# Attention with a window, then a gated convolution: another written-out order, convolution forms and PSUM banks, with ten masks on GpSimd and all but eight turns of x by DMA

## The chip, the cores and the metric

The kernel runs on one core of a Trainium2 chip. The metric is the device time of one execution in microseconds, lower is better; several executions are timed and the median counts. The engines are TensorE (PE), VectorE (DVE), ScalarE (ACT), GpSimd (POOL), and SyncE (SP), which issues nearly all DMAs here.

## The reference

Eight batches, eight heads, 576 rows, head width 64, in float32. Attention sees 32 rows to each side; its output goes into a feed-forward layer with a convolution of three taps as gate.

```python
scores = np.matmul(q, k.transpose(0, 1, 3, 2)) / np.sqrt(D)
mask = np.abs(pos[:, None] - pos[None, :]) <= 32
attn = softmax(np.where(mask, scores, -1e9))
x = np.matmul(attn, v)                       # then heads side by side: [8, 576, 512]
h = np.maximum(x @ w_in, 0.0)                # 512 -> 1024
conv = sum(conv_w[k] * hp[:, k:k + S, :] for k in range(3))   # per column, rows shifted by one
out = (h * sigmoid(conv)) @ w_out            # 1024 -> 512
```

## The kernel before

There is no loop nest and no scheduler at run time. A long string, `ORDER`, lists some 870 words, and each word calls one small function that records its instructions. The instructions of each engine run in the order in which they were recorded; semaphores hold an instruction back until its inputs are there and its buffer is free. All instructions are recorded through one helper, so nearly every row of the profile carries its line, L189; the tiles' names tell the steps apart.

A word is a step, its arguments, an engine letter (a ACT, d DVE, p POOL, t the SP queue) and, behind @, its PSUM banks. Attention works on a batch b, a half G of the heads and a half h of the rows (h=0 has four tiles of 64 rows, h=1 five):

- `lq`, `lk`, `lv` load q, k and v by SP; `cq`, `ck`, `cv` cast them to bf16 (tiles st to qb, vst to ve); `tq`, `tk` turn q and k on DVE; `vo` copies v shifted by 64 rows (ve to vo), on DVE, ACT or the queue.
- `sc` makes scores in PSUM. With the letter m the mask is added by eight more matmuls from the tile band; otherwise `mk` multiplies the exponentials by a 0/1 mask, on DVE (d) or POOL (p). `ex` is the exponential on ACT, two for each `sc`. `av` multiplies by v, `nr` normalises on DVE into xn.
- x must be turned for the next matmul: `xp` turns a block of 128 rows on PE and `xe` copies it out of PSUM, or `xt` turns it by a DMA on SP's queue.

The feed-forward part works on pieces P = 0 to 13: pieces 0 to 3 are half-width (192 rows), 4 to 13 full-width (384 rows), three to a pair of batches. In each piece m2 = 0 to 3 names a pair of 128-column groups:

- `ph` is the matmul with w_in (8 matmuls), `re` the ReLU on ACT into hT.
- `pc` starts the convolution in one of several forms. P: six matmuls with diagonal weights. A, D, S: twelve matmuls on quarter arrays. X: two scaled copies on ACT, and then `tp` adds the other two taps in four DVE instructions on the tile z. Y: half on PE, half on DVE.
- `th` is the tanh on ACT, to z in SBUF (second letter z) or in place in PSUM; `ga` multiplies by h on DVE into gT. `sw` moves halves for form S.
- `py` is the matmul with w_out (8 matmuls), `ye` copies y out of PSUM, `st` stores it.

The first feed-forward step needs attention's first batch; from there on attention of later batches and pieces of earlier ones are interleaved in `ORDER`. xT, turned x, has two buffers, each for a pair of batches; vst is one buffer for each block of v; z has four pairs of buffers.

Of the kernel before, what the change touches and what calls it, by code (L numbers as in the profile page):

```python
# [35 lines left out]
av,0,1,1@2 xe,0,0,d av,0,0,1@4 lv,1,0 ci,0,p nr,0,1,1 ph,0,2@0 ph,0,1@1 nr,0,0,1 re,0,2 lo,0 ci,3,p ph,0,0@2 re,0,1
pc,0,2,Pz@0 re,0,0 xp,0,3@1 lk,2,0 cq,1,0,p th,0,2,Pz pc,0,1,A@2 xp,0,2@4 xe,0,3,a ga,0,2,Pz ph,0,3@0 xe,0,2,a
pc,0,0,Pz@1 th,0,1,A lo,3 ck,1,0,p tq,1,0 ph,1,3@4 re,0,3 ga,0,1,A ph,1,0@5 th,0,0,Pz lq,2,0 cq,1,1,p tk,1,0 re,1,3
ph,1,2@6 re,1,0 xp,0,4@4 ga,0,0,Pz ph,1,1@5 re,1,2 lo,2 ck,1,1,p tq,1,1 xe,0,4,a sc,1,0,0,m@6+0 re,1,1 pc,1,2,P@4 lo,1
ex,1,0,0,1 cv,1,2,p tk,1,1 pc,0,3,P@5 ex,1,0,0,0 ph,2,3@0 th,1,2,P lk,2,1 cv,1,1,p th,0,3,P ga,1,2,P sc,1,1,0,d@6+2  # L40
lq,2,1 cv,1,0,a ph,2,2@1 ga,0,3,P ex,1,1,0,1 vo,1,0,d pc,1,3,Pz@4 re,2,3 ex,1,1,0,0 ph,2,1@5 lv,1,4 co,0,d re,2,2
av,1,0,0@6 th,1,3,Pz sc,1,1,1,m@0+2 mk,1,1,0,d re,2,1 pc,2,2,Pz@4 lv,1,3 ck,2,0,a ga,1,3,Pz nr,1,0,0 pc,1,1,Pz@5
th,2,2,Pz tk,2,0 th,1,1,Pz lq,3,0 co,3,p av,1,1,0@6 pc,2,3,P@4 ex,1,1,1,0 pc,1,0,P@5 ex,1,1,1,1 nr,1,1,0 ph,2,0@0
th,2,3,P lk,3,1 cq,2,0,p s6 th,1,0,P ga,1,1,Pz xp,1,0@6 xp,1,1@7 re,2,0 xe,1,0,a sc,1,0,1,m@0+2 lv,2,1 ga,2,3,P
xe,1,1,a pc,2,1,Y@6 ga,1,0,P co,2,a ph,3,3@4 ga,2,2,Pz lq,3,1 co,1,p tq,2,0 pc,2,0,Y@5 ex,1,0,1,1 ph,3,1@7 ex,1,0,1,0
tp,2,1,Y ph,3,2@2 re,3,3 lv,2,0 ck,2,1,p re,3,1 tp,2,0,Y py,0,2@4 th,2,1,Y re,3,2 ga,2,1,Y th,2,0,Y tk,2,1 lk,3,0
cq,2,1,p pc,3,3,Az@6 lk,4,0 pc,3,1,Dz@0 ye,0,2,a ga,2,0,Y cv,1,4,p py,0,1@2 th,3,1,Dz tq,2,1 th,3,3,Az lv,2,2 cv,1,3,p
ga,3,1,Dz vo,1,1,a sc,2,0,0,m@4+0 py,0,0@3 lv,2,3 cq,3,0,p ye,0,1,d ga,3,3,Az ex,2,0,0,1 lq,4,1 av,1,1,1@6 tq,3,0
ck,3,1,a py,1,0@2 st,0,1 cv,2,1,p nr,1,1,1 ex,2,0,0,0 ye,0,0,a av,1,0,1@0 tk,3,1 ye,1,0,a sc,2,0,1,d@4+6 st,0,0
cq,3,1,p ph,3,0@3 ex,2,0,1,0 nr,1,0,1 lv,2,4 pc,3,2,Pz@2 ex,2,0,1,1 re,3,0 sc,2,1,0,d@4+6 tq,3,1 th,3,2,Pz xp,1,2@0  # L50
st,1,0 ck,3,0,p xp,1,3@1 ex,2,1,0,0 xp,1,4@2 ex,2,1,0,1 pc,3,0,Pz@3 xe,1,3,d xe,1,2,a sc,2,1,1,m@4+6 mk,2,1,0,d
xe,1,4,a lk,4,1 tk,3,0 th,3,0,Pz ph,4,0@0 ex,2,1,1,1 lq,4,0 cv,2,2,p ga,3,2,Pz cv,2,0,a ex,2,1,1,0 ph,4,1@2 lv,3,0
ga,3,0,Pz ck,4,0,a mk,2,0,1,d py,1,2@4 re,4,0 tk,4,0 lv,3,2 cq,4,1,p re,4,1 lq,5,0 cv,2,3,a pc,4,0,A@0 tq,4,1 vo,2,0,t
ye,1,2,a ph,4,3@2 th,4,0,A cv,2,4,d lv,3,3 vo,2,1,d pc,4,1,P@4 lv,3,4 re,4,3 ga,4,0,A av,2,0,1@6 th,4,1,P pc,4,3,Az@2
st,0,2 ck,4,1,p nr,2,0,1 ph,4,2@0 th,4,3,Az ga,4,1,P lk,5,0 cq,4,0,p py,1,1@6 tk,4,1 re,4,2 lv,3,1 cv,3,0,p tq,4,0
pc,4,2,Pz@4 lk,5,1 cv,3,2,a ye,1,1,a ga,4,3,Az av,2,1,1@0 th,4,2,Pz sc,3,0,1,d@2+6 st,1,1 cq,5,0,p nr,2,1,1 ex,3,0,1,1
lv,4,0 av,2,1,0@4 ex,3,0,1,0 ga,4,2,Pz xp,2,4@0 xp,2,2@1 xe,2,4,a sc,3,1,1,m@2+6 xt,2,3 cv,3,3,p nr,2,1,0 py,2,0@0
ex,3,1,1,0 xe,2,2,d cv,3,4,a lv,4,2 mk,3,0,1,d ex,3,1,1,1 st,1,2 av,2,0,0@4 vo,3,1,d py,2,1@1 ye,2,0,a lv,4,3 ck,5,0,p
nr,2,0,0 lv,4,4 cv,3,1,a xp,2,0@0 ye,2,1,a xp,2,1@2 vo,3,0,d sc,3,0,0,d@4+6 xe,2,0,a py,2,2@3 xe,2,1,a tq,5,0 lk,6,1
ck,5,1,p ex,3,0,0,0 lk,6,0 ex,3,0,0,1 tk,5,0 sc,4,1,1,m@4+0 lv,4,1 cv,4,0,p ye,2,2,a av,3,1,1@6 mk,3,0,0,d lq,6,0  # L60
# [5 lines left out]
lv,5,2 lq,6,1 sc,4,0,0,d@0+6 ph,6,0@2 re,6,1 lv,6,0 ex,4,0,0,1 ex,4,0,0,0 ph,6,2@4 ga,5,1,Dz lv,5,1 cv,5,3,p re,6,0
st,2,2 th,5,2,Xz pc,5,3,Az@6 re,6,2 ph,7,0@0 lv,6,3 mk,4,0,0,d th,5,3,Az ga,5,2,Xz pc,6,0,Az@2 lv,5,4 ph,7,1@4 tq,5,1
re,7,0 th,6,0,Az lk,7,0 pc,6,2,D@0 ga,5,3,Az ph,7,2@6 tk,6,0 lq,7,0 cv,5,2,p re,7,1 pc,6,1,A@2 th,6,2,D ga,6,0,Az
py,3,0@4 re,7,2 lv,6,2 cq,6,1,p ga,6,2,D th,6,1,A pc,6,3,Az@6 py,3,1@5 ye,3,0,d th,6,3,Az ga,6,1,A st,3,0 pc,7,0,Dz@0
tq,6,0 ye,3,1,a sc,4,1,0,m@2+6 th,7,0,Dz cv,5,4,p py,3,2@4 st,3,1 ga,6,3,Az ex,4,1,0,1 vo,5,1,t ex,4,1,0,0 tq,6,1  # L70
ck,7,0,p sc,5,0,1,m@6+0 lv,6,4 ye,3,2,a av,4,1,1@2 tk,6,1 ex,5,0,1,0 cq,7,1,p st,3,2 ph,7,3@4 ex,5,0,1,1 nr,4,1,1
cq,7,0,p pc,7,1,Az@0 re,7,3 av,4,1,0@6 ck,7,1,d xt,4,3 av,4,0,0@2 th,7,1,Az py,4,1@4 cv,6,3,p nr,4,1,0 xt,4,2 cv,6,0,a
cv,5,1,d sc,5,1,1,m@0+6 nr,4,0,0 cv,6,4,p ye,4,1,a vo,5,0,t py,4,2@5 ex,5,1,1,1 ga,7,1,Az ex,5,1,1,0 xt,4,1 ga,7,0,Dz
av,5,1,1@6 ye,4,2,a xp,4,0@4 lv,6,1 sc,5,1,0,p@0+2 xe,4,0,a py,4,0@5 xt,4,4 nr,5,1,1 ex,5,1,0,0 ex,5,1,0,1 lv,7,0
tk,7,1 mk,5,1,0,p pc,7,2,Az@6 st,4,1 av,5,0,1@0 lv,7,3 th,7,2,Az ye,4,0,d pc,7,3,Az@2 st,4,2 tq,7,1 ph,8,2@4 st,4,0
# [704 lines left out]
```

## Time and profile before

| | |
|---|---|
| median of three runs | 219.03 us (217.8 to 219.38) |
| the profiled execution: its own time, its span | 217.15 us, 215.4 us |
| PE, DVE, ACT, POOL busy | 194.5, 186.9, 181.4, 62.5 us |
| granted TensorE clock | 0.999 |
| packets on the hardware DMA queue | 63184, 47.10 MB |

The span goes from the first to the last instruction; the time holds some more around it. Busy time is the union of an engine's instructions. In the profile a group's row ends with busy time and the mean duration of one, then the idle time ahead of it and what ended that; the windows' rows give from:to, length, and busy time (with count) of PE, PE's weight loads, DVE, ACT and POOL, then the clock, the DMA engines' share and GB/s.

### The profile page before, as it was taken

The page shows a single profiled execution, that of the slowest core. Times are in us where ns is not written, and L with a number is a line of the kernel's source. Part 1 is how long each engine was busy: PE and PEld are TensorE (multiplying, and loading weights), DVE is VectorE, ACT ScalarE, POOL GpSimd, SP SyncE. Part 2 cuts the span into 40 slices and gives each one's busy share as a digit, 9 for nine tenths or more (in the row PEclk, how much of TensorE's full clock was granted, in tenths as well). Part 3 has the DMA queues.
Part 4 walks back from the last instruction along what each step waited for, and adds up shares of the span by engine and source line. Part 5 has one row for each costly group of instructions (what it writes and reads, how often), then busy time and mean ns, then how long its engine had stood idle before and what let it go on. Part 6 is the DMA issues. An engine that isn't in the chain of part 4 may idle for free.

```text
span 215.4 us, 7416 instructions
## 1 busy us (share of the span) xinstructions
PE 194.5 (90%) x3113; PEld 116.0 (54%) x3134; DVE 186.9 (87%) x303; ACT 181.4 (84%) x318; POOL 62.5 (29%) x69
## 2 busy tenths in 40 slices
...
POOL 5636754565323753340336050100300000000000
...
DMA  6999999999999999999986569676236205311143
GB/s 222 315 245 394 382 287 401 332 326 337 315 375 264 324 193 348 288 242 306 262 284 186 128 158 246 138 194 185 102 94 109 97 27 158 95 34 49 53 190 146
DMA packets 63253, 47.58 MB, mean 221 GB/s; under 512 B 50012, under 2 KB 52596, under 8 KB 63220
## 3 DMA queue, kind: packets, MB, share of 16 engines
q1 hardware_dynamic: 63184, 47.10, 75.4%
...
HBM read 32.52 MB, written 9.44 MB: 195 GB/s over the span
## 4 chain that ended last, share of the span: by engine, by line
PE 63%; DVE 18%; ACT 5%; SPq 5%; issue 4%; DMA 4%; DVEq 0%
PE PS L189 63%; SPq L189 5%; DVE gT L189 3%; DVE qT L189 3%; DVE xn L189 3%; DVE kT L189 3%; DVE vo L189 3%; DMA vst<-in_v_dram 2%; DMA out_dram<-y 2%; ACT attn L189 2%; DVE attn L189 1%; ACT hT L189 1%; DVE rec L189 1%; ACT xT L189 1%; DVE xT L189 1%
## 5 line engine op out<-in xcount | busy, mean ns | idle before, releaser
L189 PE MATMUL PS<-xT,w_in_sb 128*128 128x385 bf16 (+3 forms) x448 | 70.9, 309 | 0.5 <-ACT z L189 0.4
L189 PE MATMUL PS<-w_out_sb,gT 128*128 128x512 bf16 (+1 forms) x275 | 65.5, 374 | 1.7 <-issue 0.9
L189 PEld LDWEIGHTS <-w_in_sb 128*128 128x128 bf16 x448 | 41.3, 100 | 22.4 <-issue 2.3
L189 DVE SCALAR_TENSOR_TENSOR gT<-z,hT 128x768 bf16<-128x768 f32 (+4 forms) x55 | 45.3, 838 | 5.2 <-ACT z L189 3.8
L189 ACT ACTIVATE hT<-PS 128x770 bf16<-128x770 f32 (+3 forms) x56 | 40.2, 731 | 6.8 <-PE PS L189 6.4
L189 PEld LDWEIGHTS <-gT 128*128 128x128 bf16 x296 | 26.9, 98 | 30.7 <-issue 2.8
L189 ACT ACTIVATE attn<-PS 128x512 bf16<-128x512 f32 (+1 forms) x64 | 39.0, 657 | 3.1 <-PE PS L189 2.7
L189 POOL TENSOR_SCALAR qb<-st 128x1152 bf16<-128x1152 f32 x25 | 32.2, 1288 | 30.7 <-DMA st<-in_q_dram 13.1
L189 ACT ACTIVATE z<-PS 64x384 f32<-64x384 f32 (+4 forms) x66 | 33.6, 512 | 4.4 <-PE PS L189 3.4
L189 DVE SCALAR_TENSOR_TENSOR z<-hT,conv_w_sb,z 128x384 f32<-128x384 bf16 x56 | 31.1, 618 | 0.6 <-ACT z L189 0.6
L189 PE MATMUL PS<-hT,diag_w 64*64 64x384 bf16 (+3 forms) x404 | 27.9, 307 | 0.0
L189 DVE TENSOR_TENSOR xn<-PS,rec 128x512 bf16<-128x512 f32 (+1 forms) x32 | 26.4, 824 | 1.1
L189 ACT COPY y<-PS 128x512 f32<-128x512 f32 (+1 forms) x30 | 17.3, 581 | 9.8 <-PE PS L189 8.9
L189 POOL TENSOR_SCALAR ve<-vst 128x512 bf16<-128x512 f32 x23 | 15.4, 676 | 33.3 <-DMA vst<-in_v_dram 26.0
L189 PE MATMUL PS<-qT,kT 32*128 32x64 bf16 x1152 | 15.7, 195 | 5.3 <-DVE qT L189 5.1
L189 DVE STREAM_TRANSPOSE qT<-qb 128x576 uint32<-128x576 uint32 x16 | 19.9, 1244 | 0.5 <-POOL qb L189 0.3
L189 DVE STREAM_TRANSPOSE kT<-qb 128x576 uint32<-128x576 uint32 x16 | 19.9, 1244 | 0.4 <-ACT qb L189 0.4
L189 PEld LDWEIGHTS <-diag_w 64*64 64x64 bf16 (+1 forms) x404 | 14.5, 104 | 10.4 <-issue 6.8
L189 PEld LDWEIGHTS <-kT 32*128 32x128 bf16 x1152 | 13.5, 96 | 10.8 <-issue 5.1
L189 PEld LDWEIGHTS <-attn 128*64 128x64 bf16 x640 | 13.3, 117 | 9.5 <-issue 6.3
L189 PE MATMUL PS<-ve,attn 128*64 128x65 bf16 x384 | 16.0, 203 | 2.4 <-ACT attn L189 1.4
L189 ACT ACTIVATE z<-hT,conv_w_sb 128x384 f32<-128x384 bf16 x28 | 15.7, 610 | 0.2
...
## 6 DMA issues: line engine op xcount, KB each, us to landing
...
```

Source lines behind the costliest of these rows:

```text
L189: return lambda *args, **kwargs: tc.keep_in_program_order(do(*args, **kwargs))
```

## The change

The whole of `ORDER` is replaced. The functions stay as they are, except that `pc` picks the z buffer from the piece and column group, no longer from a running count. Counted from the two strings (before, after):

| step | before | after |
|---|---|---|
| turns of x: `xp` on PE with `xe` / `xt` by DMA | 18 / 22 | 8 / 32 |
| `xe` on ACT / DVE | 14 / 4 | 7 / 1 |
| masks: in `sc` on PE / `mk` on DVE / `mk` on POOL | 15 / 15 / 2 | 16 / 6 / 10 |
| full-width convolutions: A, D, S / P / X | 23 / 3 / 14 | 16 / 5 / 19 |
| half-width: A, D / P / Y / X | 3 / 11 / 2 / 0 | 5 / 9 / 0 / 2 |
| `cq`, `ck` on ACT / DVE / POOL | 6 / 1 / 25 | 3 / 0 / 29 |
| `cv` on ACT / DVE / POOL | 10 / 7 / 23 | 5 / 5 / 30 |
| `vo` on ACT / DVE / queue | 2 / 6 / 8 | 1 / 8 / 7 |
| `co` on ACT / DVE / POOL; `dg` on ACT / DVE / POOL | 1 / 1 / 2; 3 / 4 / 1 | 0 / 0 / 4; 2 / 2 / 4 |
| `ye` on ACT / DVE | 30 / 7 | 33 / 4 |

The masks on POOL after the change are those of (b, G, h) = 2,0,1; 3,0,0; 4,0,0; 5,0,0; 5,1,0; 6,0,1; 6,1,0; 6,1,1; 7,1,0 and 7,1,1. The diff, cut to a stretch of the string that the prediction speaks of and the code:

```diff
-st,2,0 nr,3,0,0 ck,6,0,a pc,5,1,Dz@0 cv,4,1,d xp,3,0@2 re,5,2 xp,3,1@3 lk,7,1 cq,6,0,p av,4,0,1@4 xe,3,0,a xe,3,1,d
-xp,3,4@6 pc,5,2,Xz nr,4,0,1 ph,6,3@2 vo,4,0,t cq,5,1,p xe,3,4,a tp,5,2,Xz th,5,1,Dz ph,6,1@4 lq,7,1 re,6,3 cv,5,0,p
...
+mk,3,1,0,d tk,5,0 mk,4,1,1,d ph,5,1@4 sc,4,0,1,m@0+2 re,5,1 ex,4,0,1,0 ex,4,0,1,1 ph,5,2@6 av,3,1,0@0 av,3,0,0@2
+ph,5,0@4 nr,3,1,0 nr,3,0,0 lv,4,2 lv,4,4 lq,5,1 lk,6,0 lv,4,3 xt,2,4 xt,3,3 xt,3,2 xt,3,1 st,1,0 xt,3,0 lq,5,0 xt,3,4
+lv,4,0 lv,4,1 re,5,2 pc,5,2,Xz tp,5,2,Xz cv,4,4,p cv,4,2,p cq,5,1,p cv,4,3,d vo,4,1,d ck,6,0,p cq,5,0,p cv,4,0,p
+cv,4,1,p sc,4,0,0,p@0+6 pc,5,1,Pz@2 re,5,0 ex,4,0,0,0 pc,5,0,Az@4 ph,5,3@0 ex,4,0,0,1 th,5,1,Pz th,5,0,Az re,5,3
+th,5,2,Xz py,2,1@2 ye,2,1,a av,4,1,1@4 pc,5,3,Az@6 th,5,3,Az ph,6,1@0 ga,5,1,Pz tq,5,1 nr,4,1,1 tk,6,0 ga,5,0,Az
...
+mk,4,0,0,p lv,5,4 cv,5,4,p ck,5,1,p lv,5,2 vo,4,0,t lv,5,0 lv,5,3 cv,5,2,p cv,5,3,p cv,5,0,p re,6,2 ga,5,2,Xz
...
-    n_z, n_s = [0], [0]
-
     def pc(P, m2, kind, bank=None):
         w = width(P)
         if kind[0] == "A" or kind[1:] == "z":
-            i = n_z[0] % NZ
-            n_z[0] += 1
+            i = (4 * P + m2) % NZ
             z = z_all[:, 2 * i:2 * i + 2, :].rearrange("p y x -> p (y x)")
...
             if kind[0] == "S":
-                j = 2 * NZ + n_s[0] % NZS
-                n_s[0] += 1
+                j = 2 * NZ + (4 * P + m2) % NZS
```

More of the change, by code (lines that the diff above doesn't have):

```diff
@@ L36 @@
[L36 to L60, printed above, removed]
@@ L66 @@
[L66 to L75, printed above, removed]
@@ L96 @@
[L96 to L100 removed]
+lq,0,0 s5 s4 s0,d s1 s9 s3,p cw@4 lk,0,0 cq,0,0,a lq,0,1 lk,0,1 ck,0,0,p s10 lv,0,1 lv,0,2 lv,0,4 lv,0,0 lv,0,3 dg,4,d
@@ new lines @@
+cq,0,1,p dg,5,p cv,0,1,p s2 li,0 li,2 li,3 lk,1,1 lq,1,1 ck,0,1,a tq,0,0 tk,0,0 dg,3,p cv,0,4,p dg,2,p cv,0,3,p dg,7,p
+ci,0,p ci,2,p sc,0,0,0,m@4+6 sc,0,0,1,m@2+0 lk,1,0 lq,1,0 li,1 ex,0,0,0,1 ex,0,0,1,0 ex,0,0,0,0 cv,0,2,a ex,0,0,1,1
+tq,0,1 tk,0,1 s7 ci,3,p ck,1,1,p sc,0,1,1,m@2+6 sc,0,1,0,m@0+4 cq,1,1,p ck,1,0,p cq,1,0,p ci,1,p ex,0,1,1,1 ex,0,1,0,0
+ex,0,1,1,0 ex,0,1,0,1 cv,0,0,d vo,0,0,d vo,0,1,d av,0,0,0@0 av,0,1,0@2 nr,0,0,0 nr,0,1,0 av,0,1,1@4 xp,0,0@2 xp,0,1@3
+av,0,0,1@6 dg,0,d nr,0,1,1 dg,1,a nr,0,0,1 tk,1,1 xe,0,0,a xe,0,1,a dg,6,a ph,0,2@4 re,0,2 ph,0,3@5 pc,0,2,Pz@4
@@ new lines @@
+xp,0,3@1 re,0,3 xp,0,2@5 pc,0,3,Pz@3 th,0,3,Pz xe,0,2,a ph,0,0@0 tq,1,1 xe,0,3,d sc,1,1,0,m@2+6 re,0,0 th,0,2,Pz
+ex,1,1,0,1 ex,1,1,0,0 ph,1,2@5 xp,0,4@4 ph,1,0@0 lv,1,0 lv,1,2 lv,1,1 ph,1,3@6 re,1,0 re,1,3 re,1,2 cv,1,2,p tk,1,0
+tq,1,0 ph,0,1@0 sc,1,0,0,m@6+2 ph,1,1@1 pc,0,0,Pz@5 re,0,1 xe,0,4,a ex,1,0,0,1 ex,1,0,0,0 re,1,1 th,0,0,Pz pc,0,1,Pz@4
+sc,1,1,1,m@2+6 lv,1,4 lo,0 lv,1,3 lk,2,0 lq,2,0 lo,2 lo,3 lq,2,1 lk,2,1 lo,1 co,0,p cq,2,0,p ck,2,0,p co,2,p co,3,p
+cq,2,1,p ck,2,1,p co,1,p cv,1,0,d cv,1,1,d vo,1,0,d cv,1,4,d ga,0,3,Pz ga,0,2,Pz ga,0,0,Pz th,0,1,Pz ex,1,1,1,0
@@ new lines @@
+ex,1,1,1,1 av,1,0,0@0 nr,1,0,0 pc,1,2,Pz@5 av,1,1,0@2 pc,1,0,Pz@4 sc,1,0,1,m@0+6 th,1,2,Pz cv,1,3,a th,1,0,Pz ph,2,2@5
+ph,2,0@4 nr,1,1,0 ga,0,1,Pz ga,1,0,Pz vo,1,1,d pc,1,1,Az@2 ex,1,0,1,1 ex,1,0,1,0 re,2,0 th,1,1,Az xp,1,0@6 av,1,1,1@0
+xp,1,1@7 ph,2,3@4 ga,1,2,Pz nr,1,1,1 tq,2,0 pc,1,3,Az@2 av,1,0,1@0 xe,1,1,a xe,1,0,a re,2,3 re,2,2 th,1,3,Az ph,2,1@7
+ph,3,2@6 re,2,1 pc,2,0,Xz re,3,2 ph,3,1@5 ga,1,1,Az nr,1,0,1 ga,1,3,Az tk,2,0 tq,2,1 pc,2,2,Az@2 ph,3,0@1 pc,2,1,Pz@7
+pc,2,3,Pz@6 th,2,2,Az re,3,1 re,3,0 ph,3,3@4 th,2,3,Pz th,2,1,Pz xp,1,4@5 sc,2,0,0,m@0+2 py,0,2@7 tk,2,1 lq,3,0 lk,3,0
@@ new lines @@
+lv,2,2 ex,2,0,0,1 xe,1,4,a ex,2,0,0,0 ga,2,1,Pz tp,2,0,Xz pc,3,1,Xz sc,2,1,1,d@0+2 ex,2,1,1,1 ex,2,1,1,0 lv,2,3 lv,2,4
+lv,2,0 xt,1,2 lv,2,1 xt,1,3 py,0,1@5 ye,0,2,d ga,2,2,Az s6 tp,3,1,Xz ga,2,3,Pz th,2,0,Xz cv,2,2,a sc,2,0,1,p@2+0
+cv,2,3,a ex,2,0,1,1 cq,3,0,p ck,3,0,p pc,3,2,Pz@6 ex,2,0,1,0 th,3,2,Pz py,0,0@7 sc,2,1,0,d@0+2 ga,2,0,Xz tq,3,0
+py,1,0@6 mk,2,1,1,d tk,3,0 cv,2,4,p cv,2,0,p re,3,3 ex,2,1,0,1 ye,0,1,a ex,2,1,0,0 ye,0,0,a ye,1,0,a pc,3,0,Az@2
+ph,4,1@4 pc,3,3,Az@0 ph,4,2@6 th,3,0,Az th,3,1,Xz th,3,3,Az lv,3,3 lk,3,1 cv,2,1,p lv,3,4 lk,4,1 lv,3,2 lq,3,1 lv,3,0
@@ new lines @@
+st,0,1 st,0,2 lq,4,1 lk,4,0 lv,3,1 mk,2,1,0,d vo,2,1,d ga,3,2,Pz vo,2,0,d ga,3,1,Xz ga,3,0,Az av,2,1,1@2 nr,2,1,1
+ga,3,3,Az re,4,1 re,4,2 ph,4,0@0 av,2,0,0@6 mk,2,0,1,p cv,3,3,p ck,3,1,p cv,3,4,p re,4,0 cq,3,1,p av,2,0,1@4
+pc,4,1,Az@2 nr,2,0,0 nr,2,0,1 av,2,1,0@0 ph,4,3@6 pc,4,0,Pz@4 nr,2,1,0 tk,3,1 tq,3,1 th,4,1,Az re,4,3 th,4,0,Pz
+pc,4,2,Pz@2 sc,3,0,1,m@0+4 pc,4,3,Pz@6 th,4,2,Pz ex,3,0,1,0 ex,3,0,1,1 sc,3,1,1,m@0+2 py,1,2@5 th,4,3,Pz ex,3,1,1,0
+ex,3,1,1,1 sc,3,0,0,p@6+0 py,1,1@3 cv,3,2,p ck,4,1,p cq,4,1,p cv,3,0,p ck,4,0,p cv,3,1,p ye,1,2,a ex,3,0,0,0
@@ new lines @@
+ex,3,0,0,1 vo,3,0,a xt,2,2 st,0,0 ye,1,1,a xt,2,3 xt,2,1 lq,4,0 xt,2,0 lk,5,0 st,1,1 mk,3,0,0,p cq,4,0,p ga,4,1,Az
+ga,4,0,Pz vo,3,1,d ga,4,3,Pz tk,4,1 ga,4,2,Pz tq,4,1 av,3,1,1@4 av,3,0,1@0 py,2,2@6 nr,3,0,1 sc,4,1,1,d@2+0 py,2,0@7
+ex,4,1,1,0 ex,4,1,1,1 sc,3,1,0,d@2+0 ex,3,1,0,1 ex,3,1,0,0 ye,2,2,a tk,4,0 nr,3,1,1 tq,4,0 ye,2,0,d ck,5,0,p
+mk,3,1,0,d tk,5,0 mk,4,1,1,d ph,5,1@4 sc,4,0,1,m@0+2 re,5,1 ex,4,0,1,0 ex,4,0,1,1 ph,5,2@6 av,3,1,0@0 av,3,0,0@2
+ph,5,0@4 nr,3,1,0 nr,3,0,0 lv,4,2 lv,4,4 lq,5,1 lk,6,0 lv,4,3 xt,2,4 xt,3,3 xt,3,2 xt,3,1 st,1,0 xt,3,0 lq,5,0 xt,3,4
@@ new lines @@
+tp,6,1,Xz nr,4,0,1 tq,5,0 ga,5,3,Az ph,7,1@2 ph,7,2@4 th,6,0,Az th,6,1,Xz re,6,3 re,7,1 re,7,2 sc,5,0,1,m@2+6
+av,4,0,0@4 av,4,1,0@0 ex,5,0,1,1 ga,6,1,Xz tk,5,1 nr,4,0,0 pc,6,3,Pz@6 ph,7,0@4 pc,6,2,Xz ex,5,0,1,0 th,6,3,Pz
+pc,7,1,Xz nr,4,1,0 tp,6,2,Xz ga,6,0,Az sc,5,1,1,m@6+2 py,3,1@1 ex,5,1,1,0 re,7,0 ex,5,1,1,1 th,6,2,Xz pc,7,0,Xz
+ph,7,3@4 sc,5,1,0,p@2+6 py,3,0@0 ga,6,3,Pz tp,7,1,Xz ga,6,2,Xz lq,6,0 lq,6,1 lv,5,1 st,2,0 vo,5,1,t st,2,1 st,1,2
+xt,4,2 xt,4,1 st,2,2 cq,6,0,p cv,5,1,p ex,5,1,0,0 re,7,3 ex,5,1,0,1 ye,3,0,a ye,3,1,a pc,7,2,Xz mk,5,1,0,p cq,6,1,p
@@ new lines @@
+xt,4,3 lk,7,0 vo,5,0,t xt,4,0 lk,6,1 st,3,0 st,3,1 lv,6,2 av,5,0,1@2 py,3,2@5 sc,5,0,0,p@0+6 tp,7,0,Xz tq,6,0 nr,5,0,1
+py,4,0@4 ye,3,2,a ex,5,0,0,1 ex,5,0,0,0 th,7,1,Xz th,7,0,Xz av,5,1,1@6 pc,7,3,Az@0 tq,6,1 nr,5,1,1 py,4,2@2 mk,5,0,0,p
+tp,7,2,Xz ye,4,0,a th,7,3,Az ck,6,1,a py,4,1@3 av,5,1,0@6 av,5,0,0@4 ph,8,0@0 nr,5,1,0 nr,5,0,0 ga,7,1,Xz ye,4,1,a
+th,7,2,Xz ye,4,2,a re,8,0 ph,8,1@6 re,8,1 sc,6,0,1,p@2+0 ph,8,2@4 pc,8,1,Dz@6 ex,6,0,1,1 ex,6,0,1,0 re,8,2 th,8,1,Dz
+ph,8,3@0 lq,7,0 lk,7,1 xt,4,4 lv,6,0 xt,5,0 lv,6,4 xt,5,2 xt,5,3 st,3,2 lv,6,1 lv,6,3 xt,5,1 xt,5,4 st,4,1 tk,6,1
```

58 lines of the change are left out of this document (25 added, 33 removed).

## The prediction

> **What bounds the kernel now.** I read the page's span and busy shares first, then three stretches of the busy time (up to the first up-projection, up to the last attention batch, and the rest), because shares over the whole span mix a start with a steady state.
>
> ```profile
> span 215.4 us, 7416 instructions
> PE 194.5 (90%) x3113; PEld 116.0 (54%) x3134; DVE 186.9 (87%) x303; ACT 181.4 (84%) x318; POOL 62.5 (29%) x69
> ...
> POOL 5636754565323753340336050100300000000000
> ...
> DMA  6999999999999999999986569676236205311143
> ```
> ```profile
> 0.00:21.20 21.20, 8.71 (x259) 6.93 (x260) 16.27 (x44) 14.92 (x27) 11.50 (x20) 1.00 0.92 292
> 21.20:183.30 162.10, 156.81 (x2668) 94.31 (x2684) 148.18 (x226) 141.86 (x250) 51.04 (x49) 1.00 0.84 237
> 183.30:215.40 32.10, 29.02 (x195) 14.71 (x192) 22.47 (x35) 24.60 (x42) 0.00 (x0) 0.99 0.26 93
> ```
>
> In the middle stretch PE is busy 156.8 of 162.1 us, DVE 148.2 and ACT 141.9: PE sets the pace, and DVE follows 8.6 us behind it. GpSimd (POOL) is half empty and does nothing after 156 us; DMA is full until about 110 us. So PE work that is taken away is worth its time only until DVE becomes the later of the two. The sum therefore has two ways, one for PE and one for DVE, and the later one counts.
>
> **PE's part of the change.** These are groups by shape: after the bar, busy time and mean of one.
>
> ```profile
> L189 PE MATMUL PS<-hT,diag_w 64*64 64x384 bf16 x276 | 15.5, 330 | 0.0
> ...
> L189 PE MATMUL PS<-hT,diag_w 128*128 128x192 bf16 x74 | 7.8, 246 | 0.0
> ...
> L189 PE MATMUL PS<-ident,xn 128*128 128x128 bf16 x56 | 5.0, 232 | 2.4 <-DVE xn L189 2.4
> ...
> L189 PE MATMUL PS<-band 32*128 32x320 bf16 x64 | 4.1, 319 | 0.1
> ...
> L189 PE MATMUL PS<-hT,diag_w 128*128 128x384 bf16 x18 | 3.4, 326 | 0.0
> ...
> L189 PE MATMUL PS<-hT,diag_w 64*64 64x192 bf16 x36 | 1.1, 248 | 0.0
> ```
>
> Means overlap, so a matmul's price is busy time over count. Full-width convolutions in four quadrants go from 23 to 16: 7 x 12 x 56 ns = 4.7 us less. Full-width ones on whole arrays go from 3 to 5: 2 x 6 x 189 ns = 2.3 more. Half-width ones on whole arrays go from 74 matmuls to 54: 20 x 105 ns = 2.1 less. Half-width ones in quadrants go from 3 to 5: 24 x 31 ns = 0.7 more. Ten of 18 turns of x (xp) leave PE: 10 x 4 x 89 ns = 3.6 less. Masks added on PE go from 15 to 16: 8 x 64 ns = 0.5 more. Sum: 6.9 us less. The PE way is 215.4 - 6.9 = 208.5 us of span, if nothing else waits.
>
> **DVE's part.**
>
> ```profile
> L189 DVE SCALAR_TENSOR_TENSOR z<-hT,conv_w_sb,z 128x384 f32<-128x384 bf16 x56 | 31.1, 618 | 0.6 <-ACT z L189 0.6
> L189 DVE SCALAR_TENSOR_TENSOR gT<-z,hT 128x768 bf16<-128x768 f32 x32 | 30.9, 984 | 2.3 <-DMA z<-z 1.1 <-ACT z L189 1.0
> ...
> L189 DVE SCALAR_TENSOR_TENSOR gT<-z,hT 128x384 bf16<-128x384 f32 x13 | 8.8, 684 | 2.7 <-ACT z L189 2.7
> ...
> L189 DVE COPY vo<-ve 64x1040 bf16<-64x1040 bf16 x12 | 8.1, 675 | 0.7 <-issue 0.4
> ...
> L189 DVE TENSOR_TENSOR attn<-attn,mask 128x1280 bf16<-128x1280 bf16 x8 | 6.5, 817 | 0.2 <-ACT attn L189 0.2
> ...
> L189 DVE SCALAR_TENSOR_TENSOR gT<-PS,hT 128x384 bf16<-128x384 f32 x10 | 5.3, 549 | 1.1 <-ACT PS L189 1.0
> ...
> L189 DVE TENSOR_TENSOR attn<-attn,mask 128x1024 bf16<-128x1024 bf16 x7 | 5.1, 724 | 0.1
> ...
> L189 DVE CAST xT<-PS 128x512 bf16<-128x512 f32 x4 | 2.8, 689 | 1.9 <-PE PS L189 1.9
> ...
> L189 DVE SCALAR_TENSOR_TENSOR PS<-hT,conv_w_sb,PS 128x192 f32<-128x192 bf16 x4 | 1.6, 420 | 0.1
> ```
>
> Form X gives two convolution taps of both columns to DVE; five more full-width steps are 20 x 618 ns = 12.4 us. Eight half-width taps replace four: 4 x 420 ns = 1.7. Nine masks leave (six of 1280, three of 1024 columns): 6 x 817 + 3 x 724 ns = 7.1 less. Twelve small casts and evacuations leave (xe 3, ye 3, cv 2, dg 2, ck 1, co 1); at the xT row's 689 ns they are 8.3 less. Two vo steps of two copies come from ACT and the queue: 4 x 675 ns = 2.7. Gates: +4 x 984, +7 x 684, -9 x 549, and ten short ones gone, priced by the nearest row at 549: 1.7 less. Sum: 0.3 us less. What was taken off DVE is put back on it as taps.
>
> **ACT** is no bound: it gains at most 14 scaled copies and loses more.
>
> ```profile
> L189 ACT ACTIVATE z<-hT,conv_w_sb 128x384 f32<-128x384 bf16 x28 | 15.7, 610 | 0.2
> ...
> L189 ACT CAST qb<-st 128x1152 bf16<-128x1152 f32 x6 | 7.1, 1186 | 0.0
> ...
> L189 ACT CAST xT<-PS 128x512 bf16<-128x512 f32 x10 | 5.7, 592 | 1.6 <-PE PS L189 1.6
> ```
>
> 14 x 610 ns = 8.5 more at most; seven xT copies (4.1), three k casts (3.6), and smaller casts and tanh pieces less. I take ACT as hidden behind the other two.
>
> **What POOL takes over.**
>
> ```profile
> L189 POOL TENSOR_SCALAR qb<-st 128x1152 bf16<-128x1152 f32 x25 | 32.2, 1288 | 30.7 <-DMA st<-in_q_dram 13.1 <-DVE qT L189 8.5 <-DMA st<-in_k_dram 4.9
> ...
> L189 POOL TENSOR_SCALAR ve<-vst 128x512 bf16<-128x512 f32 x23 | 15.4, 676 | 33.3 <-DMA vst<-in_v_dram 26.0 <-PE PS L189 7.3
> ...
> L189 POOL TENSOR_TENSOR attn<-attn,mask 128x1024 bf16<-128x1024 bf16 x2 | 4.3, 2126 | 14.1 <-ACT attn L189 14.1
> ```
>
> Ten masks instead of two: four more of 1024 columns (8.5 us) and four of 1280, estimated at 2126 x 1.25 ns each (10.6). Then 4 casts of q or k (5.2), 7 of v (4.7), and two w_out casts and three diagonals at 1288 ns (6.4). POOL goes from 62.5 to 97.9 us, which fits in the span; but it is not free, because POOL and DVE hold each other up:
>
> ```profile
> 4.79 1.66 DVE L189 TENSOR_TENSOR diag_w<-ident,conv_w_sb 128x384 bf16<-128x384 bf16 x2
> ```
> ```profile
> 134.72 2.12 DVE L189 SCALAR_TENSOR_TENSOR z<-hT,conv_w_sb,z 128x384 f32<-128x384 bf16 x3
> ```
> ```profile
> 64.33 1.84 DVE L189 COPY vo<-ve 64x1040 bf16<-64x1040 bf16 x2
> ```
> ```profile
> 64.74 1.15 POOL L189 TENSOR_SCALAR qb<-st 128x1152 bf16<-128x1152 f32 x1 [0.72 <-DMA st<-in_q_dram]
> ```
>
> The two vo copies take 1.84 us together; the shortest of that shape takes 0.42. The second began beside a POOL cast and ended just after it. Taking every DVE instruction against the shortest of its shape, 16 of them (the first two rows hold the first and the last) are 8.5 us too long, each beside a POOL instruction: masks, taps, gates that read z, SBUF copies. Transposes, normalisations and PSUM reads are never longer. That is r = 8.5 / 62.5 = 0.136 us of DVE per us of POOL.
>
> The Trainium skill (SBUF — State Buffer, "Who interferes with whom") says that a DVE instruction with two SBUF inputs contends with a GpSimd one that reads SBUF, and that of DVE's 2-port modes and GpSimd the first to issue blocks the other fully. The rows above agree, 1.4 us where 0.42 would do. By that rule, if all the added POOL work fell on such DVE work, DVE would lose 35.4 us more and the sum below would be 243 us; no such collision of every instruction is seen here.
>
> So r is the unknown cost. From below: both POOL masks of before stood beside transposes, normalisations or a y copy and cost DVE nothing, so r = 0.10 is possible if masks are placed so again. From above: after the change POOL works beside the tap-heavy second half, so r = 0.22. I take 0.136, the row's own.
>
> **DVE way.** DVE idles 28.5 us: 4.9 in the first stretch, 8.8 behind its last gate, 14.8 between.
>
> ```profile
> 205.27 0.96 DVE L189 SCALAR_TENSOR_TENSOR gT<-z,hT 128x768 bf16<-128x768 f32 x1 [0.20 <-ACT z L189]
> 211.69 0.42 DVE L189 COPY y<-PS 128x256 f32<-128x256 f32 x1 [5.47 <-PE PS L189]
> ```
>
> From 183.3 us to the last gate's end at 206.2 it idles only 0.9 of 22.9 us, 4%; I let it idle that much of some 185 us, 7.4. Work without delays is 186.9 - 8.5 - 0.3 = 178.1. The way is 178.1 + 4.9 + 8.8 + 7.4 = 199.2, and 97.9 r on top: 13.3 at r = 0.136, so 212.5 us. It is later than PE's 208.5 by 4.0.
>
> **Turns of x by DMA.** Each is 1.26 us of issue on the queue, and lands later:
>
> ```profile
> L189 SPq DMA_TRANSPOSE xT<-xn x22: 1171/1257/2313, 73.4 to 188.2; - x22
> ```
> ```profile
> DMA to landing us min/median/max: 2.3/3.2/5.7
> ```
> ```profile
> 90.85 1.48 PE L189 MATMUL PS<-xT,w_in_sb 128*128 128x385 bf16 x8
> ...
> 93.27 0.62 PE L189 MATMUL PS<-ident,xn 128*128 128x128 bf16 x8 [0.33 <-DVE xn L189]
> ```
>
> Most have over 10 us of other PE work before their block is read. The tight one is piece 6: its first block (ph,6,1) needs xt,3,1 and xt,3,0. From the last AV matmul at 90.85 to the turn on PE was 2.4 us; now come two issues of 1.26, a store's issue between them, and 2.3 to 5.7 us from the second one's issue to landing, 6.5 to 9.9 in all. PE has some 8 us between (two ph of 1.5, one py, three convolutions, scores): a wait of 0 to 2. Behind the same turns stand lv,4,0 and lv,4,1, then vo,4,0; av,4,0,0 waits for that, another 0 to 2. PE's slack of 4.0 us against DVE hides both; without that cover they cost up to 4.
>
> **Sum.** The span is 212.5, 2.9 less than 215.4; the profiled execution's own time 217.15 becomes 214.25. The runs' median, 219.03, is 0.87% above the profiled execution, so the forecast is 216.1 us.
>
> **Rivals.** (1) Slower: the shared port. If r reaches 0.22, the DVE way is 199.2 + 21.5 = 220.7, 5.3 over now, and the median 224.4. It decides from r = 0.19 on. For it: taps and z gates, which are held up, grow, and masks of over 2 us hold longest. Against it: POOL's two old masks cost nothing. (2) No gain, the change undone by what it moves: nine masks save 7.1 us of DVE, and the added POOL work takes it back at r = 0.17: 199.2 + 16.6 = 215.8, a median of 219.4. (3) PE keeps the pace and DVE's idle time goes: 208.5, a median of 212.0. Against it: DVE would have to run 97% full from 21 us on. (4) The turns by DMA wait in a full queue, 4 us on top of (2): 223.5. For it: DMA's nines until 110 us.
>
> **How the numbers follow.** The forecast's case has 0.37, (3) 0.08, (2) 0.20, (1) 0.23, (4) 0.12. About 1% is what a measurement of this kernel can tell from no change. Faster: 0.45; same: 0.20; slower: 0.35. The range goes from a little under (3), 210.5, to a little over (1), 225.0; without the slower cases it would be 211 to 219.
>
> **What would show it.** Right: PE busy about 188, DVE 190 to 193 with 12 to 15 us of over-long instructions, POOL near 98, waits for DVE's z or gT growing ahead of PE. Wrong: DVE's over-long instructions above 18 us (rival 1), PE waits of over 1 us for xT or vo landings (rival 4), ACT busier than DVE, or a start in which the first up-projection comes over 2 us later than 21.2.

## The result, and the profile after

The changed kernel takes 235.88 us (median of four runs, 233.54 to 236.81). Beside it the kernel before took 219.2 us (217.8 to 221.34). The ratio is 1.077, with a 95% interval of 1.066 to 1.088. The forecast was 216.1 us and the range ended at 225.0, so the change is slower than anything the prediction allowed for. The profiled execution took 236.11 us. Executions of one kernel now and then fall into a state that is some per cent slower: medians here are of all runs of a kernel, ratios of the fast runs alone, against the kernel before measured beside them.

The page of the changed kernel, its busy shares, GpSimd's slices, the clock's slices and the shares of the chain that ended last:

```profile
span 234.4 us, 7227 instructions
...
PE 196.4 (84%) x3034; PEld 113.8 (49%) x3034; DVE 210.8 (90%) x294; ACT 173.8 (74%) x310; POOL 104.6 (45%) x101
...
POOL 5685634974836955068508618851505400000000
PEclk9999999999999999999999999798899999999999
...
DVE 43%; PE 37%; ACT 7%; issue 5%; DMA 5%; SPq 1%; ACTq 0%; DVEq 0%
```

DVE went from 186.9 to 210.8 us with nine instructions fewer, and it is now the largest share of the chain (18% before, 43% now). GpSimd now works until 187 us; before, it stopped at 156. The same three stretches, cut at the first up-projection and 1.4 us ahead of the last normalisation, as before:

```profile
0.00:21.87 21.87, 10.27 (x266) 7.30 (x267) 15.96 (x33) 12.07 (x21) 14.29 (x32) 1.00 0.90 282
21.87:193.50 171.63, 149.16 (x2528) 88.16 (x2526) 164.74 (x212) 130.88 (x236) 90.29 (x70) 0.98 0.83 224
193.50:234.40 40.90, 36.93 (x256) 18.34 (x249) 30.11 (x49) 30.88 (x55) 0.00 (x0) 0.99 0.26 93
```

The start costs 0.7 us and the end 8.8 us more, because work has moved behind the last attention batch (36.9 us of PE against 29.0). In the middle PE is idle for 22.5 us (5.3 before), while DVE is busy 164.7 of 171.6 us. What DVE does longer stands in the groups by shape, and with it GpSimd's groups:

```profile
L189 DVE SCALAR_TENSOR_TENSOR z<-hT,conv_w_sb,z 128x384 f32<-128x384 bf16 x76 | 54.9, 786 | 0.1
...
L189 DVE SCALAR_TENSOR_TENSOR gT<-z,hT 128x768 bf16<-128x768 f32 x36 | 40.9, 1166 | 0.9 <-ACT z L189 0.6
L189 POOL TENSOR_SCALAR qb<-st 128x1152 bf16<-128x1152 f32 x29 | 37.8, 1306 | 43.7 <-DMA st<-in_q_dram 27.9 <-DVE kT L189 9.6 <-DMA st<-in_k_dram 3.8
...
L189 POOL TENSOR_SCALAR ve<-vst 128x512 bf16<-128x512 f32 x30 | 26.1, 876 | 12.4 <-DMA vst<-in_v_dram 11.6 <-ACT z L189 0.8
...
L189 POOL TENSOR_TENSOR attn<-attn,mask 128x1024 bf16<-128x1024 bf16 x6 | 14.3, 2380 | 14.6 <-ACT attn L189 13.8 <-POOL attn L189 0.8
...
L189 POOL TENSOR_TENSOR attn<-attn,mask 128x1280 bf16<-128x1280 bf16 x4 | 11.4, 2853 | 4.0 <-ACT attn L189 4.0
```

A full-width tap takes 786 ns on average (618 before), a gate 1166 (984), although each does the same as before. GpSimd's own instructions stretch as well: a v cast takes 876 ns (676), a mask of 1024 columns 2380 (2126). The timeline shows where the time goes (start, length, engine, instruction):

```profile
104.70 5.65 DVE L189 SCALAR_TENSOR_TENSOR z<-hT,conv_w_sb,z 128x384 f32<-128x384 bf16 x4
...
105.23 2.42 POOL L189 TENSOR_TENSOR attn<-attn,mask 128x1024 bf16<-128x1024 bf16 x1
...
141.94 5.17 DVE L189 SCALAR_TENSOR_TENSOR gT<-z,hT 128x768 bf16<-128x768 f32 x2
...
143.00 3.29 POOL L189 TENSOR_TENSOR attn<-attn,mask 128x1280 bf16<-128x1280 bf16 x1
```

The first two rows are one pair, the last two another. Four taps take some 2.3 us when nothing is in their way; here they take 5.65. The second of them began at 105.58, just behind the mask's start, and ended at 108.05, 0.4 us after the mask. Two gates take some 1.9 us; here 5.17, and the second began at 143.75, behind the mask's start, and ended 0.8 us after the mask. Taken against the shortest of its shape, as in the prediction, 42 DVE instructions are 35.3 us too long in all (16 and 8.5 us before). What an instruction is too long by is called its hold from here on. PE waits for what comes behind these instructions on DVE. Its waits for DVE's normalised rows and gates (us in total, times, longest) were, in the kernel before, where it had none for a gate:

```profile
PE PS L189 <- DVE xn L189: 4.0, 5, 1.2
```

and are, in the changed one:

```profile
PE PS L189 <- DVE xn L189: 12.9, 11, 3.5
PE PS L189 <- DVE gT L189: 4.4, 2, 3.0
```

No wait of PE ends with a mask of GpSimd, so nothing shows that the masks themselves came late.

### The profile page after: what moved, and what is told of

Read it like the earlier page. It is cut to its first block, busy times and chain, and to the rows that moved or that the text cites. A ratio compares the mean times of both kernels' runs of the same rounds, so it can differ in the third digit from the quotient of the medians.

```text
span 234.4 us, 7227 instructions
## 1 busy us (share of the span) xinstructions
PE 196.4 (84%) x3034; PEld 113.8 (49%) x3034; DVE 210.8 (90%) x294; ACT 173.8 (74%) x310; POOL 104.6 (45%) x101
## 4 chain that ended last, share of the span: by engine, by line
DVE 43%; PE 37%; ACT 7%; issue 5%; DMA 5%; SPq 1%; ACTq 0%; DVEq 0%
PE PS L189 37%; DVE z L189 13%; DVE gT L189 12%; DVE xn L189 5%; DVE qT L189 4%; DMA st<-in_k_dram 3%; DVE kT L189 3%; DVE vo L189 3%; ACT attn L189 2%; DVE attn L189 2%; ACT z L189 2%; DMA out_dram<-y 2%; ACT hT L189 1%; DVE rec L189 1%; ACT y L189 1%
## 5 line engine op out<-in xcount | busy, mean ns | idle before, releaser
L189 PE MATMUL PS<-w_out_sb,gT 128*128 128x512 bf16 (+1 forms) x296 | 68.1, 377 | 7.9 <-DVE gT L189 4.4
L189 DVE SCALAR_TENSOR_TENSOR gT<-z,hT 128x768 bf16<-128x768 f32 (+2 forms) x62 | 60.5, 1002 | 1.4 <-ACT z L189 0.9
L189 DVE SCALAR_TENSOR_TENSOR z<-hT,conv_w_sb,z 128x384 f32<-128x384 bf16 (+1 forms) x84 | 58.4, 758 | 0.1
L189 POOL TENSOR_SCALAR qb<-st 128x1152 bf16<-128x1152 f32 x29 | 37.8, 1306 | 43.7 <-DMA st<-in_q_dram 27.9
L189 ACT ACTIVATE attn<-PS 128x512 bf16<-128x512 f32 (+1 forms) x64 | 39.0, 656 | 11.4 <-PE PS L189 11.4
L189 POOL TENSOR_TENSOR attn<-attn,mask 128x1024 bf16<-128x1024 bf16 (+1 forms) x10 | 25.7, 2569 | 18.6 <-ACT attn L189 17.8
L189 POOL TENSOR_SCALAR ve<-vst 128x512 bf16<-128x512 f32 x30 | 26.1, 876 | 12.4 <-DMA vst<-in_v_dram 11.6
L189 PE MATMUL PS<-hT,diag_w 64*64 64x384 bf16 (+3 forms) x336 | 25.2, 311 | 1.6 <-DVE xn L189 0.9
L189 ACT ACTIVATE z<-z 128x768 f32<-128x768 f32 (+1 forms) x21 | 17.0, 813 | 9.9 <-DVE z L189 9.8
L189 ACT ACTIVATE z<-hT,conv_w_sb 128x384 f32<-128x384 bf16 (+1 forms) x42 | 22.6, 595 | 1.9 <-DVE gT L189 1.8
L189 PE MATMUL PS<-vo,attn 128*64 128x65 bf16 x256 | 15.4, 206 | 3.5 <-DVE vo L189 3.5
```

The lines of the kernel that those rows point to most:

```text
L189: return lambda *args, **kwargs: tc.keep_in_program_order(do(*args, **kwargs))
```

## The experiments

**Is it the ten masks?** In the first three kernels the masks of the changed kernel leave GpSimd and all else stays.

e2_masks_pe, the masks on PE:

```diff
-sc,4,0,0,p@0+6 ... mk,4,0,0,p      (ten of these)
+sc,4,0,0,m@0+6
```

> The changed kernel with the same ten masks added on PE (eight more matmuls each, 5 us of PE in all) and no mk step for them. Theory (shared port): DVE's over-long time falls from 35.3 to about 18, DVE busy about 193, span about 217, median about 218 to 220. Rival (order and queue): the median stays within 2% of 236, since PE gets more work and nothing of the order changes.

Measured: 217.56 us (216.45 to 222.45) against 218.69; ratio 0.998 [0.993, 1.003]. Eighty more matmuls on PE, and some 18 us less than with the masks on GpSimd; the forecast's 218 to 220 is missed by half a microsecond. Its page:

```profile
span 216.8 us, 7355 instructions
...
PE 193.2 (89%) x3092; PEld 114.6 (53%) x3114; DVE 194.3 (90%) x294; ACT 173.5 (80%) x310; POOL 77.4 (36%) x91
```

DVE has the same 294 instructions as in the changed kernel and is busy 16.5 us less. Some 18 us of holds are left beside casts, and 1 us beside two of GpSimd's diagonals.

e1_masks_dve and e5_masks_dve_placed, the masks on DVE, first where the string has them and then where GpSimd had begun them. Among DVE's own steps seven of the ten masks then stand earlier, two later and one in the same place; the order of every other step on its engine stays:

```diff
-mk,4,0,0,p
+mk,4,0,0,d      (ten of these; in e5 the words also stand elsewhere in the string)
```

> The changed kernel with its ten POOL masks given to DVE, at the same places of the order. Theory (shared port: POOL's masks hold DVE's taps and gates): of the 35.3 us by which DVE instructions are too long, the 17.0 beside masks go, and ten masks of about 0.75 us come on DVE (7.5): DVE busy about 201, span about 225, median about 227. Rival (the new order and its waits on the queue cost the time, POOL is only busy beside it): DVE gains 7.5 us of work and the median is 236 or above.

> The changed kernel with its ten POOL masks on DVE, each put into DVE's order at the moment at which POOL began it in the profile of the changed kernel (the earlier run had them wherever the string named them, and DVE waited 5.9 us in front of one, PE 6.9 us for others). Theory (shared port): DVE busy about 200, median 224 to 229. Rival (the order costs the time): median above 232, as in the earlier run.

Measured: 232.95 us (ratio 1.066 [1.056, 1.077]) and 227.73 us (1.052 [1.043, 1.060]). e1 missed its 227: DVE runs its instructions in order and stood 5.9 us ahead of one mask, waiting for the exponential, and PE waited 6.9 us for masks. With the masks placed anew e5 fell into its forecast of 224 to 229. So even on DVE, where they cost 7.6 us of its time (six at 724 ns, four at 817), the masks are cheaper than on GpSimd, by 8 us between the medians (ratios 1.052 and 1.077).

**Do masks alone do it?** e3_before_masks_pool puts eight DVE masks of batches 4, 6 and 7 of the kernel before on GpSimd:

```diff
-mk,6,1,0,d
+mk,6,1,0,p      (eight of these)
```

> The kernel before with eight of its DVE masks (batches 4, 6 and 7) given to POOL, everything else as it was. Theory (shared port): 6.1 us of work leave DVE, but some 20 us of masks on POOL at 0.66 us of delay per us put 13 us back, so DVE gets 7 us longer and the median is 224 to 230. Rival (order and queue): masks on POOL alone do no harm, the median is 219 or a little less.

Measured: 227.31 us, ratio 1.036 [1.026, 1.047]. DVE loses eight masks' worth of work and the kernel becomes slower. Six of the masks hold a tap or a gate, by 1.7 to 2.4 us each, 11.9 us in all; one of them in the timeline:

```profile
144.21 3.31 DVE L189 SCALAR_TENSOR_TENSOR gT<-z,hT 128x768 bf16<-128x768 f32 x1 [0.56 <-DMA z<-z]
...
144.10 2.61 POOL L189 TENSOR_TENSOR attn<-attn,mask 128x1280 bf16<-128x1280 bf16 x1
```

The gate of 0.94 us takes 3.31. e4_before_z_index gives the kernel before the one change in the code, the new choice of the z buffer:

```diff
-            i = n_z[0] % NZ
-            n_z[0] += 1
+            i = (4 * P + m2) % NZ
```

> The kernel before with the other choice of the z buffers alone. Both theories: no change within 1%, 217 to 221, unless the buffers come round in a worse order, which would show as waits of ACT for DVE's z.

Measured: 219.22 us, ratio 0.997 [0.984, 1.010]. It is not the buffers.

**What about the masks does it?** Three kernels add GpSimd work that nobody needs to the kernel before, behind GpSimd's last step, from 156 us on, when GpSimd is otherwise idle: ten multiplications of 1280 columns, twenty memsets, twenty casts.

```diff
+gpsimd.tensor_tensor(out=scr, in0=mask, in1=mask, op=ALU.mult)                 # e7_pool_reads, x10
+gpsimd.memset(scr, 0.0)                                                        # e8_pool_writes, x20
+gpsimd.tensor_scalar(out=scr, in0=src, scalar1=1.0, scalar2=0.0, op0=ALU.mult, op1=ALU.add)   # e10_pool_casts, x20
```

> The kernel before, and behind POOL's last step (at about 155 us) ten more POOL multiplications of the mask tile by itself into a dead tile, 1280 columns each, some 2.65 us. Nothing waits for them. Theory (shared port): they hold DVE's taps and gates in 156 to 183 us, 0.6 us of delay per us, 10 to 17 us in all, and the median is 228 to 236. Rival (POOL beside DVE costs nothing by itself, only steps that wait for POOL do): 219 within 1%.

> The same, with twenty POOL memsets of the same dead tile (about 1.3 us each) in place of the ten multiplications: POOL is as busy but reads nothing. If it is the reading through a shared way that holds DVE, then taps and gates are not held, and the median is 219 within 1%. If any POOL instruction holds them: 228 or above.

> The kernel before, with twenty more GpSimd instructions behind its last step that do nothing for the result: casts of 1152 float32 to bf16 of one SBUF input, the form of the casts of q and k (1.3 us each, 26 us in all, from about 156 us on). Ten multiplications of two inputs for the same 26 us made the kernel 8.7% slower, twenty memsets left it as it was. Theory (a read with one input holds DVE at about a third of the price of one with two, 0.2 to 0.3 us of DVE per us): 5 to 8 us slower, 223 to 227, holds of under 1 us each. Rival A (any read of SBUF by GpSimd holds DVE alike): 234 to 238. Rival B (casts cost nothing, what was seen beside them came from other things): 218 to 220.

Measured: the multiplications 236.11 us (1.087 [1.080, 1.095]), the memsets 217.06 us (0.999 [0.995, 1.003]), the casts 231.84 us (1.060 [1.052, 1.068]). The stretch from 155 to 186 us, first of the kernel before, then with the multiplications, then with the memsets (length, busy time of PE, PE's loads, DVE, ACT and POOL, then the clock):

```profile
155.00:186.00 31.00, 30.68 (x426) 15.89 (x422) 29.09 (x51) 27.93 (x48) 0.60 (x1) 1.00 0.39 104
```
```profile
155.00:186.00 31.00, 16.94 (x179) 8.22 (x179) 30.92 (x21) 12.77 (x23) 26.33 (x11) 0.78 0.19 51
```
```profile
155.00:186.00 31.00, 30.68 (x486) 16.09 (x480) 28.55 (x49) 27.85 (x49) 25.35 (x21) 1.00 0.37 96
```

DVE is "busy" 29 to 31 us in all three, but with the multiplications it gets through 21 instructions in place of 51, and PE through 179 in place of 426. With the memsets GpSimd is as busy, and nothing changes. Row by row, with the multiplications and with the memsets:

```profile
164.10 10.45 DVE L190 SCALAR_TENSOR_TENSOR z<-hT,conv_w_sb,z 128x384 f32<-128x384 bf16 x4
...
163.44 10.69 POOL L190 TENSOR_TENSOR vst<-mask 128x1280 bf16<-128x1280 bf16 x4
```
```profile
164.51 2.20 DVE L190 SCALAR_TENSOR_TENSOR z<-hT,conv_w_sb,z 128x384 f32<-128x384 bf16 x4
...
162.98 12.16 POOL L190 MEMSET vst<- 128x1280 bf16 x10
```

Four taps take 10.45 us beside four multiplications: one tap to each. Beside memsets they take 2.20. So GpSimd holds DVE with instructions that read SBUF and not with those that only write it. The casts were to tell whether the second input matters; I had expected a third of the multiplications' price, 223 to 227 us, and that was wrong, though 231.84 also stays under the 234 to 238 of an equal price:

```profile
159.87 5.74 DVE L192 SCALAR_TENSOR_TENSOR z<-hT,conv_w_sb,z 128x384 f32<-128x384 bf16 x4
...
161.04 5.58 POOL L192 TENSOR_SCALAR vst<-vst 128x1152 bf16<-128x1152 f32 x4
```

Here too each GpSimd instruction holds one tap, 0.89 us each; 18 of the 20 casts held something, 15.7 us in all, where the ten multiplications held 19.3. In this stretch a cast costs DVE 0.68 us per us of its undisturbed length (15.7 of 20 x 1.16), nearly a multiplication's 0.83 (19.3 of 10 x 2.32). So where casts are cheap in the kernel before, it is for their place and not for their kind.

**Does a hold end with the GpSimd instruction?** Two kernels cut the reads into quarters: the masks of the changed kernel, and the useless multiplications.

```diff
-        {"d": vector, "p": gpsimd}[e].tensor_tensor(out=attn, in0=attn, in1=mask[:, 0:4 * n], op=ALU.mult)
+        if e == "p":                                                            # e12_masks_in_parts
+            for i in range(4):
+                c = slice(i * n, (i + 1) * n)
+                gpsimd.tensor_tensor(out=attn[:, c], in0=attn[:, c], in1=mask[:, c], op=ALU.mult)
+            return
+        vector.tensor_tensor(out=attn, in0=attn, in1=mask[:, 0:4 * n], op=ALU.mult)
...
-        gpsimd.tensor_tensor(out=scr, in0=mask, in1=mask, op=ALU.mult)
+        for i in range(4):                                                      # e13, against e7
+            c = slice(320 * i, 320 * (i + 1))
+            gpsimd.tensor_tensor(out=scr[:, c], in0=mask[:, c], in1=mask[:, c], op=ALU.mult)
```

> The changed kernel with each of its ten GpSimd masks issued as four multiplications of 256 or 320 columns in place of one of 1024 or 1280; the work is the same. In the changed kernel each of the ten held one DVE instruction for all that was left of it, 17 us in all. Theory (a GpSimd read holds a DVE instruction that was issued behind it until that GpSimd instruction ends, and no longer): no hold is longer than one part, about 0.6 us; with a tap of 0.6 us between two parts the holds come to about 0.4 us per us of masks, 9 to 12 us in all, and the kernel gets 4 to 8 us faster than the changed one: 228 to 232. Rival (the two share the reading time by its length, however it is cut): 17 us of holds or more, 235 to 238.

> The kernel before, with the ten useless GpSimd multiplications of 1280 columns behind its last step (236.1 us, 8.7% slower; each held one DVE instruction, 19 us in all) issued as forty of 320 columns. Theory (a hold ends with the GpSimd instruction): holds of 0.6 us at most, some 10 to 13 us in all, 227 to 231. Rival (by length of reading): 234 to 238. Second rival (short instructions slip in between DVE's and cost next to nothing): 219 to 223.

Measured: 227.73 us (1.052 [1.045, 1.058]) where the changed kernel has 235.88 (1.077), and 231.86 us (1.056 [1.046, 1.065]) where whole multiplications have 236.11 (1.087). Both times lie just outside their forecasts, the first below and the second above. No hold beside a part is longer than 0.60 us (masks) or 0.53 us (multiplications); beside whole ones they reached 2.42 and 2.17 us. So a hold does end with the GpSimd instruction. But there are more of them: in all, the masks' holds fall from 17.1 to 11.4 us and the multiplications' only from 19.3 to 15.0 (I had said 10 to 13). The rows of the quartered masks, and GpSimd's groups:

```profile
144.28 7.50 DVE L189 SCALAR_TENSOR_TENSOR z<-hT,conv_w_sb,z 128x384 f32<-128x384 bf16 x8
...
143.60 7.77 POOL L189 TENSOR_TENSOR attn<-attn,mask 128x320 bf16<-128x320 bf16 x8
```
```profile
L189 POOL TENSOR_TENSOR attn<-attn,mask 128x256 bf16<-128x256 bf16 x24 | 23.0, 987 | 12.1 <-ACT attn L189 12.1
L189 POOL TENSOR_TENSOR attn<-attn,mask 128x320 bf16<-128x320 bf16 x16 | 16.6, 1068 | 2.9 <-ACT attn L189 2.9
```

Eight taps and eight quarters in 7.5 us: the engines take turns. The masks take GpSimd 39.6 us now, against 25.7 whole, partly because each quarter waits for a tap as each tap waits for a quarter.

**Is there more to gain?** Three kernels start from e2. e6_v_casts_act moves 23 casts of v from GpSimd to ACT; e9_all_masks_pe puts the six masks that DVE still has on PE; e11_x_turns_pe puts the ten turns of x back on PE.

```diff
-cv,4,0,p
+cv,4,0,a                              (e6: 23 of these, batches 3 to 7)
-sc,6,0,0,d@2+4 ... mk,6,0,0,d
+sc,6,0,0,m@2+4                        (e9: six of these)
-xt,3,1
+xp,3,1@6 ... xe,3,1,a                 (e11: ten of these)
```

> The changed kernel with its ten POOL masks on PE, and 23 casts of v (batches 3 to 7) moved from POOL to ACT at the moments at which POOL began them. Theory (shared port): POOL falls by 14 to 20 us, DVE's over-long time from about 18 to 13 or 14, ACT rises to about 188, and the median is 212 to 216, under the kernel before. Rival (ACT becomes the bound, or ACT waits in front of casts whose v has not landed): 218 or above.

> The changed kernel with its ten GpSimd masks on PE, and the six masks that DVE still has (2,1,1; 2,1,0; 3,1,0; 4,1,1; 6,0,0; 7,0,0) on PE as well. Theory: DVE's work is the bound; DVE loses 4.7 us of busy time (194.3 to 189.6), PE gains 6 x 8 x 64 ns = 3.1 us (193.2 to 196.3); the two ways meet, median 214 to 217. Rival: PE is already the bound once the masks are gone from GpSimd, and the kernel gets 1 to 3 us slower than with ten masks moved (217.6): 218.5 to 221.

> The changed kernel with its ten GpSimd masks on PE, and the ten turns of x that the change moved to the DMA queue (1,2; 1,3; 2,0; 2,1; 2,2; 2,4; 3,0; 3,1; 3,4; 4,0) back on PE with a copy on ACT each, so that eight turns by DMA are left in the first half. Theory: the turns by DMA were hidden and cost nothing; PE gains 3.6 us and ACT 5.9 us of work, median 217 to 222 (217.6 with the turns by DMA). Rival (the turns waited in the queue, and something behind them too): up to 4 us faster, 213.5 to 216.5.

e6 missed: 221.23 us, ratio 1.018 [1.012, 1.024]. DVE did get shorter, but ACT's busy time rose by 11 us, and PE's waits for the exponentials grew from 3.1 to 4.9 us. The profile is of an execution of 224.94 us and the three others took 220.6 to 221.42, so it only suggests that ACT costs the gain.

```profile
PE 195.7 (88%) x3092; PEld 116.5 (52%) x3114; DVE 190.5 (85%) x294; ACT 184.4 (83%) x333; POOL 58.6 (26%) x68
```

e9 gave 218.58 us, ratio 0.998 [0.994, 1.003], just above the rival's lower end: DVE falls to 187.0 us and nothing comes of it, because PE (194.2) is the longer one again. e11 gave 221.25 us, 1.003 [0.997, 1.009], within the theory's 217 to 222: the turns by DMA were hidden, as priced. No version here beats the kernel before by more than a measurement can tell.

## Why the prediction was wrong, point by point

**The frame held, one of its terms did not.** The DVE way was work without delays, plus idle time at start, end and between, plus the holds. Measured, these are 175.5 us of work (178.1 predicted), 23.6 of idle time (21.1) and 35.3 of holds (13.3), together the span of 234.4 (212.5). Of the miss of 21.9 us, 22.0 are the holds; the work, 2.6 shorter, and the idle time, 2.5 longer, cancel, which is luck.

**The failed step is r, DVE's delay per us of GpSimd work**: 0.136 taken, 0.22 as the upper bound, 0.337 measured (35.3 / 104.6). GpSimd's own work was sized nearly right (97.9 predicted; 104.6 includes the time for which DVE held it). This is rival (1), the shared port, which had 0.23; it came far beyond its price, because r was taken for a constant. Even the upper bound, 0.22, had no row behind it, although the vo copy among the prediction's rows was held until GpSimd's cast had ended. The reads of GpSimd against the holds, counted for every GpSimd instruction that reads a large tile (a DVE tap, gate from z, SBUF copy or mask was issued while it ran; it held one for over 0.15 us; the holds' sum; counts shift by up to three, sums by half a microsecond, with what is taken as such an instruction):

| kernel | GpSimd reads | met such a DVE instruction | held it | holds, us |
|---|---|---|---|---|
| before | 56 | 21 | 13 | 7.5 |
| changed: casts and weights | 67 | 36 | 31 | 17.7 |
| changed: the ten masks | 10 | 10 | 10 | 17.1 |
| changed, masks on PE | 67 | 38 | 34 | 18.3 |
| before with ten multiplications: these alone | 10 | 10 | 10 | 19.3 |
| before with twenty memsets: these alone | 20 | 17 | 0 | 0 |

A GpSimd read that met such an instruction held it in 13 of 21 cases before and in 41 of 46 in the changed kernel. A hold there is the rest of the GpSimd instruction less 0.1 to 0.2 us, in all but one case. Where there was no hold, the read mostly had 0.3 us or less left; one gate of the changed kernel, at 56.36 us, ran without one beside a v cast with 1.0 us left, and why is not known. Transposes, normalisations and instructions that read PSUM began beside GpSimd reads some 50 times before and 40 times after, and were never over 0.07 us too long. What the prediction needed was not a mean per us but two counts: how many reads meet a tap or gate, and how long each read is. The first mean came from a kernel in which 35 of 56 reads met none, its two masks among them. After the change all ten masks met one and cost 1.7 us each, and casts with weights went from 7.5 to 17.7 us: more of them (67 for 54), and more of them that met one (36 for 21).

**The rule that was set aside.** The Trainium skill (SBUF — State Buffer, "Who interferes with whom") has a DVE instruction with two SBUF inputs contend with GpSimd's reads, and says of DVE's 2-port modes and GpSimd that whoever issues first blocks the other fully. The prediction's sum by it, 35.4 us more for DVE and 243 us, was put away as "no such collision of every instruction"; measured are 26.8 us more and 235.9 us. Taken for every added read it counts too much for the casts (31 of 67 held something), and it is right for the masks (ten of ten). The same section also says that GpSimd work which only writes does not contend with a DVE instruction of two SBUF inputs; the memsets agree (0.999).

**The other steps.** PE's work was to fall by 6.9 us, to 187.6. With the ten masks on PE (e2, eighty matmuls at 64 ns, 5.1 us) it is 193.2, so 188.1 without them: the sum of parts was right. In the changed kernel, where PE starves, the same matmuls count 196.4 us; the lower clock told of below can be a part of that, but was not separated. ACT fell, 173.8 from 181.4, and is no bound, as said. The first up-projection came at 21.87 us, within the 2 us. Rival (2), no gain, is what the change comes to without GpSimd's masks (e2). Rival (3) needed DVE nearly free of holds. Rival (4), the turns waiting in the queue, did not happen: e11 gains nothing by taking ten turns off the queue. The tight places of the changed kernel on PE:

```profile
99.64 0.68 PE L189 MATMUL PS<-hT,diag_w 64*64 64x384 bf16 x12
100.25 1.00 PE L189 MATMUL PS<-xT,w_in_sb 128*128 128x386 bf16 x5
...
113.92 0.19 PE L189 MATMUL PS<-ve,attn 128*64 128x65 bf16 x1 [0.21 <-ACT hT L189]
```

Piece 6 begins at 100.25 right behind a convolution, and the AV of batch 4 that needed the late copy of v (av,4,0,0) waits 0.21 us, for a ReLU and not for that copy. Nor is any landing of xT or vo among the waits of PE.
